# Larger loads, an earlier last K and one end barrier in a load-bound attention decode kernel

## The chip, the cores and the metric

The kernel runs on one core of one Trainium2 chip. Times are device microseconds of that core, medians of several executions. Executions mostly agree within 0.3%, but a few runs are 1 to 2 us longer at an unchanged granted clock. In the views, PE is the matmul engine (PEld its weight load), DVE the vector engine, ACT the scalar engine, POOL the general one, SP the engine that issues the large loads; a q behind a name (SPq) is the engine's instruction sequencer.

## The reference, cut to what matters

```python
# x [4,1,640]; 32 heads of 192; window of the last 2048 keys of 8192; bf16
xn = layernorm(x)
q = xn @ wq                                   # [640, 6144]
o = softmax(q . k_window * 192**-0.5) @ v_window   # for each of 4 x 32 heads
out = x + o @ wo + (silu(xn @ w1) * (xn @ w3)) @ w2
```

K and V of the window are 201 MB, wq and wo 7.9 MB each, w1, w3 and w2 2 MB each: 223 MB are read once for four output rows.

## The kernel before: the parts that the change touches

All large loads go through one queue (`nc.sync`), in program order. Its first load is moved ahead of the start barrier.

```python
def first_load_first(nc):
    for f in nc.python_module().functions:
        head, body = f.blocks[0], f.blocks[1]
        sp = mybir.EngineType.SP
        ...   # the first DMA of this queue goes from body into head, before its drain
```

The loads at the start: `x` on the other queue, wq in three transfers that lie in the three V buffers, then the first two K heads.

```python
    x_sb = const.tile([B, D], BF16, name="x_sb")
    nc.scalar.dma_start(out=x_sb[:], in_=A_x.rearrange("b s d -> (b s) d"))
    wq_v = A_wq.rearrange("(p kc) n -> p kc n", kc=KC)          # KC = 5
    for k0 in range(0, KC, 2):                                  # 2, 2, 1 rows a partition
        n = min(2, KC - k0)
        wt = vpool.tile([P, 2, H * Dh], BF16, tag="vt")
        nc.sync.dma_start(out=wt[:, 0:n, :]..., in_=wq_v[:, k0:k0 + n, :]...)
        ...
    for h in range(KBUFS):                                      # KBUFS = 2
        load_k(h)
```

From x come the layer norm, its transpose, q (60 matmuls with wq), and with q the DVE products with K. Each head has four products (`mult`). The third K load needs the buffer of the first K, so it is issued only after the first head's fourth product:

```python
    for h in range(H):
        u0, ul = h * GQ, h * GQ + GQ - 1                        # GQ = 4
        if h >= KBUFS:
            add((h - KBUFS + 1) * GQ, 0, load_k, h)
        if h < H - 2:
            add(u0 + 2, 0, load_v, h)
```

w1's last 64 rows ("low" rows) are loaded in four small transfers laid out so that only a few of the 16 DMA engines carry them. The end:

```python
    for h in range(H - 2, H):
        add(NU - 6, 0, load_v, h)
    add(NU - 6, 0, w2_load, 0)                                  # W2C: 4, 4, 3, 1 rows
    add(NU - 6, 0, w2_load, 1)
    add(NU - 6, 0, wo_load, NG - 2)                             # wo in groups of 4 heads
    add(NU - 6, 0, wo_load, NG - 1)
    add(NU - 6, 0, w2_load, 2)
    add(NU - 6, 0, w2_load, 3)
```

## Time and profile before

| | before |
|---|---|
| time | 525.7 us |
| span of the profiled run, its time | 523.8, 525.59 us |
| load queue, share of 16 engines | 99.2% |
| DVE, PE busy | 65%, 69% |

From the page of the kernel before: the mean busy share of the DMA engines in 40 slices of 13 us (tenths), what they moved, and the queues with packets, MB and share.

```profile
DMA  9999999999999999999999999999999999999996
GB/s 389 422 443 425 433 431 432 428 433 432 430 435 428 437 418 446 424 437 426 434 434 429 432 434 429 435 427 435 425 437 434 427 437 431 430 434 425 441 418 275
...
q1 hardware_dynamic: 11868, 222.96, 99.2%
q8 instruction: 15, 0.25, 0.2%
```

The engines are full from the second slice to the last but one, so the kernel is bound by its loads. The Trainium skill ("DMA: Bandwidth & Descriptors", Where 436 GB/s comes from) puts the ceiling at 435 GB/s; the middle of this trace, at 428 to 435 in stretches of 20 us, agrees.

From the timeline of the kernel before: start, duration, engine, line, operation; in brackets the idle time before it and what ended it.

```profile
0.00 1.69 SPq L148 DMA_DIRECT2D wt<-in_A_wq_dram  x3
0.79 0.55 ACTq L142 DMA_DIRECT2D x_sb<-in_A_x_dram  x1
...
6.68 0.48 DVE L177 CAST xf<-x_sb 4x640 f32<-4x640 bf16 x1 [3.80 <-DMA x_sb<-in_A_x_dram]
...
41.62 0.54 SPq L125 DMA_DIRECT2D kt<-in_A_k_cache_dram  x1
```

x is 5 KB and is asked for at 0.79 us, but the first operation on it starts at 6.68. The third K load is issued at 41.62.

The end, from the same timeline:

```profile
518.65 0.38 DVE L369 STREAM_TRANSPOSE oT<-og 128x192 bf16<-128x192 bf16 x1
...
519.21 0.98 PE L264 MATMUL acc<-wo_t,oT 128*4 128x320 bf16 x12 [0.47 <-DMA wo_t<-in_A_wo_dram]
520.38 0.71 PE L264 MATMUL acc<-w,hT 128*4 128x320 bf16 x8 [0.19 <-DMA w<-in_B_w_dram]
521.12 0.48 DVE L542 CAST res<-acc 4x320 bf16<-4x320 f32 x1 [2.10 <-PE acc L264]
```

PE waits for loads (wo, then w2) at the very end, and the result copy follows at once. The records of line 569 hold the end barriers: operation, count, shortest/median/longest ns, first and last start.

```profile
L569 SPq DRAIN  x3: 7/7/13, 523.0 to 523.4; - x3
L569 POOLq EVENT_SEMAPHORE  x4: 17/17/17, 523.1 to 523.7; - x4
L569 POOLq EVENT_SEMAPHORE_RANGE_CLEAR  x1: 96/96/96, 523.4 to 523.4; - x1
```

The first barrier stands before the semaphore clear at 523.4, the second after it, up to 523.7.

The trace has a record of every DMA packet, without the engine's number. Weighing each with its steady spacing (about 4.5 ns plus its bytes at 27.2 GB/s, read from packets that follow each other on one engine) gives the work done per engine up to any moment. The **mean lag** is the clock minus that work; it grows only while engines stand still or restart. In the kernel before it is 1.91 us at 40 us, 2.81 at 500. The growth is about that of the instruction fetches: in the packet records those of 16 KB (15 of them) each hold their DMA engine up by about 1.4 us, of which the fetch's own bytes are 0.6 us of work, so that all 15 make 0.75 us spread over 16 engines (an estimate from these figures); five smaller fetches of 8 KB add some more.

### The profile page before, as it was taken

Reading aid. Unit: us, or ns where it says so; the run is one execution under the profiler, and the core shown is the slowest. Engines: PE = TensorE matmul, PEld = TensorE weight load, DVE = VectorE, ACT = ScalarE, POOL = GpSimd, SP = SyncE. Lnnn points to the kernel's source line nnn. Section 1 sums busy time; section 2 is a strip of 40 time slices with the busy share of each in tenths; the row PEclk is TensorE's granted clock in tenths of the full one; section 3 lists DMA queues with packets and bytes.
Section 4 is the critical chain, followed back from the end, with each engine's and each line's share of the span. In section 5 each row is a group of like instructions: output and inputs, shape, how many; then the busy total and the mean of one; then the engine's idle time right before and its main releaser. Section 6 shows DMA issues by size and latency. Waiting matters only on the chain.

```text
span 523.8 us, 4820 instructions
## 1 busy us (share of the span) xinstructions
PE 361.8 (69%) x2336; PEld 75.9 (14%) x1643; DVE 340.9 (65%) x413; ACT 55.8 (11%) x176; POOL 5.6 (1%) x12
## 2 busy tenths in 40 slices
PE   0965866887668776667547768586686876675685
PEld 0100111121111111111111111111111111111122
DVE  3268853687656767577646877466667766667671
ACT  2111111111001110101100111001101110011111
POOL 4000000000000000000000000000000000000000
PEclk9979886898878998789997988889878898889988
DMA  9999999999999999999999999999999999999996
GB/s 389 422 443 425 433 431 432 428 433 432 430 435 428 437 418 446 424 437 426 434 434 429 432 434 429 435 427 435 425 437 434 427 437 431 430 434 425 441 418 275
DMA packets 11904, 223.26 MB, mean 426 GB/s; under 512 B 1332, under 2 KB 1608, under 8 KB 3052
## 3 DMA queue, kind: packets, MB, share of 16 engines
q1 hardware_dynamic: 11868, 222.96, 99.2%
q8 instruction: 15, 0.25, 0.2%
q14 instruction: 5, 0.04, 0.0%
q10 hardware_dynamic: 16, 0.01, 0.0%
HBM read 222.96 MB, written 0.01 MB: 426 GB/s over the span
## 4 chain that ended last, share of the span: by engine, by line
DMA 60%; PE 20%; DVE 15%; ACT 3%; issue 1%; SPq 1%
DMA kt<-in_A_k_cache_dram 44%; PE ps L288 11%; DMA w<-in_B_w_dram 11%; DVE pr L277 10%; DMA vt<-in_A_v_cache_dram 5%; PE po L361 4%; PE qps L243 3%; DVE sc L296 2%; ACT ex L324 1%; DVE z L332 1%; DMA x_sb<-in_A_x_dram 1%; PE mt L318 1%; ACT L324 0%; ACT negm L321 0%; PE mt L305 0%
## 5 line engine op out<-in xcount | busy, mean ns | idle before, releaser
L288 PE MATMUL ps<-pr,idb 128*128 128x512 bf16 x768 | 214.7, 422 | 137.6 <-DVE pr L277 137.5
L277 DVE TENSOR_TENSOR pr<-kt,qbc 128x3072 bf16<-128x3072 bf16 x128 | 223.5, 1746 | 104.0 <-DMA kt<-in_A_k_cache_dram 104.0
L296 DVE TENSOR_REDUCE sc<-ps 128x16 f32<-128x512 f32 x128 | 87.1, 681 | 2.7 <-PE ps L288 2.6
L340 PE MATMUL o_ps<-vt,z 128*8 128x384 bf16 x1024 | 60.5, 380 | 0.2 <-DVE z L332 0.2
L361 PE MATMUL po<-o_sb,sel_w 128*32 128x192 f32 x128 | 49.2, 518 | 0.6 <-ACT o_sb L343 0.6
L340 PEld LDWEIGHTS <-z 128*8 128x8 bf16 x1024 | 26.2, 95 | 98.8 <-issue 89.2
L332 DVE TENSOR_TENSOR z<-ex,mask_b 128x256 bf16<-128x256 bf16 x32 | 13.5, 423 | 38.6 <-ACT ex L324 38.6
L343 ACT COPY o_sb<-o_ps 128x384 f32<-128x384 f32 x32 | 15.3, 478 | 196.9 <-PE o_ps L340 196.9
L313 ACT ACTIVATE gneg<-gmax 1x128 f32<-1x128 f32 x32 | 9.8, 308 | 162.8 <-DVE gmax L310 162.8
L305 PEld LDWEIGHTS mt<-idf,lmax 128*1 128x1 f32 x32 | 3.2, 101 | 127.5 <-issue 125.5
L361 PEld LDWEIGHTS po<-o_sb,sel_w 128*32 128x32 f32 x128 | 13.8, 130 | 29.4 <-issue 27.9
L288 PEld LDWEIGHTS <-idb 128*128 128x128 bf16 x124 | 12.0, 97 | 39.3 <-issue 32.8
L318 PEld LDWEIGHTS mt<-ones_ff,gneg 1*128 1x128 f32 x64 | 9.6, 186 | 47.1 <-issue 43.7
L243 PE MATMUL qps<-wt,xnT 128*128 128x512 bf16 x59 | 14.9, 412 | 0.1
L318 PE MATMUL mt<-ones_ff,gneg 1*128 1x1 f32 x64 | 12.3, 259 | 0.7 <-ACT gneg L313 0.7
L321 ACT COPY negm<-mt 128x1 f32<-128x1 f32 x32 | 5.1, 159 | 70.4 <-PE mt L318 70.4
L310 DVE TENSOR_REDUCE gmax<-mt 1x4 f32<-1x128 f32 x32 | 8.8, 274 | 5.8 <-PE mt L305 5.8
L348 PEld LDWEIGHTS po<-rsum,tot_w 128*32 128x32 f32 x64 | 4.4, 108 | 51.5 <-ACT ex L324 35.4
L249 DVE CAST qbc<-qps 128x512 bf16<-128x512 f32 x6 | 3.8, 684 | 11.7 <-PE qps L243 11.7
L324 ACT ACTIVATE ex<-sc,negm 128x64 bf16<-128x64 f32 x32 | 11.1, 348 | 1.0
L305 PE MATMUL mt<-idf,lmax 128*1 128x128 f32 x32 | 10.9, 340 | 0.0
L199 PE MATMUL xnT_ps<-idb,xn 4*128 4x4 bf16 x5 | 0.4, 178 | 13.4 <-DVE xn L194 13.4
(74 smaller groups left out, 84.4 us busy)
## 6 DMA issues: line engine op xcount, KB each, us to landing
kt<-in_A_k_cache_dram SPq DMA_DIRECT2D x32, 3072.0 KB, 19.1
vt<-in_A_v_cache_dram SPq DMA_DIRECT2D x32, 3072.0 KB, 25.5
wo_t<-in_A_wo_dram SPq DMA_DIRECT2D x8, 960.0 KB, 20.7
wt<-in_A_wq_dram SPq DMA_DIRECT2D x2, 3072.0 KB
w<-in_B_w_dram SPq DMA_DIRECT2D x1, 1920.0 KB
wt<-in_A_wq_dram SPq DMA_DIRECT2D x1, 1536.0 KB, 19.5
w<-in_B_w_dram SPq DMA_DIRECT2D x1, 1536.0 KB
w<-in_B_w_dram SPq DMA_DIRECT2D x2, 640.0 KB
```

What stands on the lines that cost most here:

```text
L243: nc.tensor.matmul(qp[:], lhsT=xnT[:, kc].rearrange("p a b -> p (a b)"), rhs=wq_rows[kc][:, (c0 + i) * QC:(c0 + i + 1) * QC], start=(kc == ...
L277: nc.vector.tensor_tensor(out=pr[:], in0=kts[h][:, g * JQ:(g + 1) * JQ, :], in1=qbc[:, h * Dh:(h + 1) * Dh].unsqueeze(1).to_broadcast([P, ...
L288: nc.tensor.matmul(ps[:], lhsT=idb[:], rhs=pr[:, :, kk * DD:(kk + 1) * DD], start=(kk == 0), stop=(kk == NK - 1))
L296: nc.vector.tensor_reduce(out=scs[h][:, g * JQ:(g + 1) * JQ], in_=pss.pop(u)[:], axis=AX.X, op=ALU.add)
L305: nc.tensor.transpose(out=mt[0:1, 0:P], in_=chs[h][0][:], identity=idf[:])
L313: nc.scalar.activation(out=gneg[:], in_=gmax[:].unsqueeze(1).to_broadcast([1, PB, B]), func=ACTF.Copy, scale=-SCALE)
L318: nc.tensor.matmul(mt[:, P:P + 1], lhsT=gneg[:].rearrange("o p b -> o (p b)"), rhs=ones_ff[:], start=True, stop=True)
L324: nc.scalar.activation(out=ex[:], in_=scs.pop(h)[:], func=ACTF.Exp, bias=negm[:, 0:1], scale=SCALE, accum_out=rsum[:])
L332: nc.vector.tensor_tensor(out=z[:], in0=ex[:].unsqueeze(2).to_broadcast([P, NJ, B]), in1=mask_b[:].unsqueeze(1).to_broadcast([P, NJ, B]), ...
L340: nc.tensor.matmul(o_ps[c * CT:c * CT + 2 * B, :], lhsT=z[:, 2 * jj:2 * jj + 2, :], rhs=vt[:, 2 * jj:2 * jj + 2, :], start=(jj < 4), stop= ...
L343: nc.scalar.copy(out=o_sb[:], in_=o_ps[:])
L361: nc.tensor.matmul(po[sl, 0:Dh], lhsT=sel_w[:, par].rearrange("p a b -> p (a b)"), rhs=o_sb[:, par * Dh:(par + 1) * Dh].rearrange("p (r i) ...
```

## The change

The intent: fewer and larger transfers (wq in two, w2 in one, wo by eight heads instead of four), a last K that does not come behind the third-last V so that the last softmax is done early, a simpler layout of w1's low rows (72 rows in two transfers), and the second end barrier left out.

```diff
+def one_end_barrier(nc):
+    ...  # deletes what follows the semaphore clear in the end block, but for one drain of Pool
-    HG: int = 4,
+    HG: int = 8,
+    FG: int = 4,
@@ wq, in one tile that holds all three V buffers
-    for k0 in range(0, KC, 2):
-        n = min(2, KC - k0)
-        wt = vpool.tile([P, 2, H * Dh], BF16, tag="vt")
+    wq_t = v_all[:, 0:KC * H * Dh].rearrange("p (k n) -> p k n", k=KC)
+    for k0, k1 in ((0, 3), (3, KC)):
@@ the last K into a V buffer, the last V into a K buffer
+        kt = k_buffer() if h < H - 1 else v_buffer()
+        vt = v_buffer() if h < H - 1 else k_buffer()
+    early = {H - 1: (NU - 10, -1)}
@@ low rows of w1
-    for n in range(4):
-        add(4 + 2 * n, 1, w1_low, n)
+    for n in range(2):
+        add(5 + 3 * n, 1, w1_low, n)
@@ the end
-    add(NU - 6, 0, w2_load, 0)  # and 1, 2, 3, with two wo_load between
+    WOC = [0, RPP - 5, RPP - 2, RPP]
+    add(NU - 6, 0, w2_load)
+    for i0, i1 in zip(WOC, WOC[1:]):
+        add(NU - 6, 0, wo_load, NG - 1, i0, i1)
+        add(e, 6, ge_proj, NG - 1, i0, i1, True)
...  # cut: layouts of po, og, oT for eight heads; w1's matmuls
```

## The prediction

> **What bounds the kernel.** The DMA engines. The page's queue part puts the load queue at 99.2% of the 16 engines' time; the stretch table shows 428 to 435 GB/s in every 20 us from 40 to 500 us. The Trainium skill ("DMA: Bandwidth & Descriptors", Where 436 GB/s comes from) gives a ceiling of 435 GB/s; the trace agrees. DVE (65%) and PE (69%) have slack.
>
> From the packet records: 24,576-byte packets start 908 ns apart on an engine, 7,680 ones 287, 1,280 ones 52: about 4.5 ns per packet plus bytes at 27.2 GB/s; a semaphore packet takes 6 ns. With packets weighed so, the engines' mean work lags the clock by 1.9 us from 3 us on (start, fixed), by 0.9 us more from 15 instruction fetches, by nothing else until 517.5. Then engines run out one by one: four with few fetches at 517.2 to 518.6, the others at 519.6 to 520.5. After the last landing (about 520.8) come two projection matmuls (0.30), the copy (0.48), the store and two end barriers, up to 523.8; 1.8 us more lie outside the span.
>
> **What the change does.** It saves no bytes; it adds 24.6 KB (eight w1 rows loaded twice), 0.06 us.
> - Larger packets: wq 128 fewer, wo 256, w2 384: 48 per engine at 4.5 ns, 0.22 us; 7 fewer transfers at 6 ns, 0.04 us. All on the critical path: every engine is full.
> - Low rows of w1: 72, not 64, on the same three engines. Those get about 0.3 us more work; they end at 519.6 to 520.3 now, so they just reach the others' end. At most 0.1 us lost.
> - Last K ahead of three V: same bytes, so the last landing stays. The last K lands about 7 us earlier, its softmax is done before the last V lands (about 511 us), and the transposed output is ready near 517.5 instead of 519.03. Before, that chain already waits for data (0.5 us for wo, 0.2 for w2): safety, not time.
> - Scaling and transposing 384 columns, not 192: 0.4 us longer, inside that slack.
> - After the last landing four matmuls, not two: 0.1 us more (8 took 0.71, 2 took 0.30).
> - Second end barrier: its records run from about 523.45 to 523.75; 0.25 to 0.35 us saved.
>
> Sum: -0.26 +0.06 +0.1 -0.3 = -0.4 us.
>
> **Prediction: 525.3 us, range 524.5 to 525.9.** Faster by over 2%: 0.01; within 2%: 0.98; slower by over 2%: 0.01.
>
> **What would show it.** Load queue still 99%, span about 523.4; 768 fewer large packets; the middle at 428 to 435 GB/s. In the chain of waits the last DMA is a wo piece landing near 520.6, then four matmuls; PE waits for wo, not for the transposed output. After the semaphore clear only one drain.
>
> **What would make it wrong.** Instruction fetches (the skill's "Runtime: NRT & Kernel Launch", Instruction fetch mechanics, says 16 KiB blocks; the trace has 15 of 16,384 bytes) delay single engines by about 1.4 us each; if the shifted program puts them on other engines or near the end, the last landing moves by some tenths. Buffers shared between K, V and wq, or the single wo buffer, could make the in-order load queue wait long enough to starve the engines; I estimate over 8 us of backlog there. If the order near the end exposes the last head's chain, PE would wait for the transposed output.

## The result, and the profile after

The changed kernel takes **526.56 us** (median of six runs, 526.16 to 528.43) against 525.72 (525.61 to 526.16). The ratio is 1.0019 with a 95% interval of 1.0004 to 1.0034: slower by a fifth of a percent, where 525.3 was predicted.

The page and the start and end of the timeline of the changed kernel, in the order of those of before:

```profile
DMA  9999999999999999999999999999999999999996
GB/s 385 426 443 423 432 427 434 427 437 433 432 433 433 431 427 437 424 441 430 429 434 427 439 425 433 431 431 435 431 431 431 431 431 437 429 430 433 428 433 260
...
q1 hardware_dynamic: 10974, 222.98, 99.1%
q8 instruction: 15, 0.25, 0.2%
```

```profile
0.00 1.11 SPq L177 DMA_DIRECT2D v_all<-in_A_wq_dram  x2
0.79 0.54 ACTq L173 DMA_DIRECT2D x_sb<-in_A_x_dram  x1
...
8.10 0.48 DVE L206 CAST xf<-x_sb 4x640 f32<-4x640 bf16 x1 [5.22 <-DMA x_sb<-in_A_x_dram]
...
43.02 0.54 SPq L156 DMA_DIRECT2D kt<-in_A_k_cache_dram  x1
...
517.32 0.58 DVE L401 STREAM_TRANSPOSE oT<-og 128x384 bf16<-128x384 bf16 x1
...
519.17 1.75 PE L295 MATMUL acc<-wo_t,oT 128*4 128x320 bf16 x20 [0.93 <-DMA wo_t<-in_A_wo_dram]
...
521.08 0.44 PE L295 MATMUL acc<-wo_t,oT 128*4 128x320 bf16 x4 [0.17 <-DMA wo_t<-in_A_wo_dram]
...
521.55 0.48 DVE L549 CAST res<-acc 4x320 bf16<-4x320 f32 x1 [3.65 <-PE acc L295]
```

The barriers' records of the changed kernel:

```profile
L576 SPq DRAIN  x2: 7/10/13, 523.5 to 523.5; - x2
L576 POOLq EVENT_SEMAPHORE  x2: 17/17/17, 523.6 to 523.6; - x2
L576 POOLq EVENT_SEMAPHORE_RANGE_CLEAR  x1: 96/96/96, 523.8 to 523.8; - x1
```

What is as predicted: the load queue is as full, 792 data packets fewer (the 768 predicted, of wq, wo and w2, and 24 of w1's low rows), the transposed output is ready 1.1 us sooner (its start plus duration: 517.90 against 519.03), PE waits for wo and not for it, and only a drain follows the clear. What is not: x is first used 1.4 us later, and with it the third K load is issued 1.4 us later; the last load packet ends at 520.77 us instead of 520.49; and 2.16 us instead of 1.79 lie outside the span. For the profiled pair (526.16 and 525.59, a difference of 0.57) the sum closes:

| step | before | changed | difference |
|---|---|---|---|
| last load packet ends | 520.49 | 520.77 | +0.28 |
| from there to the result copy | 0.63 | 0.78 | +0.15 |
| from the copy to the end of the span | 2.68 | 2.45 | -0.23 |
| outside the span | 1.79 | 2.16 | +0.37 |

But this profiled run is the fastest of the six. The median is 0.4 us further up, and something that this trace does not show must make the others slow.

### The profile page after: what moved, and what is told of

It reads as the page before. It is cut to its first block, busy times and chain, and to the rows that moved or that the text cites. A ratio compares the mean times of both kernels' runs of the same rounds, so it can differ in the third digit from the quotient of the medians. Undisturbed runs are those within 1.5% of the kernel's fastest.

```text
span 524.0 us, 4763 instructions
## 1 busy us (share of the span) xinstructions
PE 356.6 (68%) x2327; PEld 74.7 (14%) x1633; DVE 339.6 (65%) x398; ACT 55.9 (11%) x176; POOL 5.5 (1%) x11
## 4 chain that ended last, share of the span: by engine, by line
DMA 61%; DVE 18%; PE 18%; ACT 2%; issue 1%; SPq 0%
DMA kt<-in_A_k_cache_dram 52%; DVE pr L309 12%; PE ps L320 9%; DMA wo_t<-in_A_wo_dram 7%; PE po L393 4%; PE qps L274 3%; DVE sc L328 2%; DMA x_sb<-in_A_x_dram 1%; DVE z L364 1%; ACT ex L356 1%; PE mt L350 1%; ACT L356 0%; PE mt L337 0%; ACT negm L353 0%; DVE xn L223 0%
## 5 line engine op out<-in xcount | busy, mean ns | idle before, releaser
L320 PE MATMUL ps<-pr,idb 128*128 128x512 bf16 x768 | 211.7, 417 | 144.1 <-DVE pr L309 144.1
L309 DVE TENSOR_TENSOR pr<-kt,qbc 128x3072 bf16<-128x3072 bf16 x124 | 216.5, 1747 | 104.6 <-DMA kt<-in_A_k_cache_dram 104.6
L372 PE MATMUL o_ps<-v_all,z 128*8 128x384 bf16 x992 | 54.9, 366 | 0.4 <-DMA v_all<-in_A_v_cache_dram 0.4
L274 PE MATMUL qps<-v_all,xnT 128*128 128x512 bf16 x59 | 15.0, 415 | 0.1
```

Of the source, the lines that this page charges most:

```text
L274: nc.tensor.matmul(qp[:], lhsT=xnT[:, kc].rearrange("p a b -> p (a b)"), rhs=wq_rows[kc][:, (c0 + i) * QC:(c0 + i + 1) * QC], start=(kc == ...
L309: nc.vector.tensor_tensor(out=pr[:], in0=kts[h][:, g * JQ:(g + 1) * JQ, :], in1=qbc[:, h * Dh:(h + 1) * Dh].unsqueeze(1).to_broadcast([P, ...
L320: nc.tensor.matmul(ps[:], lhsT=idb[:], rhs=pr[:, :, kk * DD:(kk + 1) * DD], start=(kk == 0), stop=(kk == NK - 1))
L372: nc.tensor.matmul(o_ps[c * CT:c * CT + 2 * B, :], lhsT=z[:, 2 * jj:2 * jj + 2, :], rhs=vt[:, 2 * jj:2 * jj + 2, :], start=(jj < 4), stop= ...
```

## The experiments

Thirteen runs were made (one of them the changed kernel, unaltered) on four chips, each beside runs of the kernel before on the same chip; all gave right results. The key numbers, the first from the timelines, the lag and the last packet from the packet records of the profiled run, the time as the median of the runs:

| kernel | first op on x | third K issued | mean lag at 40 / 100 us | last packet | time | before |
|---|---|---|---|---|---|---|
| before | 6.68 | 41.62 | 1.91 / 2.05 | 520.49 | 525.72 | |
| changed | 8.10 | 43.02 | 2.01 / 2.15 | 520.77 | 526.56 | 525.72 |
| changed, again | 8.43 | 42.01 | 2.11 / 2.26 | 520.59 | 526.53 | 525.70 |
| before, one end barrier | 6.93 | 41.97 | 1.91 / 2.07 | 520.42 | 525.81 | 525.61 |
| changed, two end barriers | 7.67 | 43.43 | 2.09 / 2.64 | 521.90 | 526.80 | 525.61 |
| changed, wq in three | 6.88 | 41.93 | 1.94 / 2.08 | 520.52 | 525.88 | 525.61 |
| changed, one last wo row | 8.32 | 43.44 | 2.13 / 2.82 | 521.79 | 527.20 | 525.61 |
| changed, x first | 5.53 | 41.31 | 2.01 / 2.15 | 520.56 | 525.98 | 525.64 |
| before, wq in two | 8.29 | 44.49 | 2.02 / 4.03 | 523.36 | 527.99 | 525.64 |
| wq in three, w1 back | 6.87 | 40.80 | 1.89 / 2.03 | 520.11 | 526.12 | 525.64 |
| wq in three, last K back | 6.97 | 42.02 | 1.89 / 2.05 | 520.26 | 525.87 | 525.64 |
| before, x late | 10.04 | 44.03 | 1.98 / 3.07 | 522.41 | 527.69 | 525.71 |
| mended | 4.26 | 40.69 | 1.93 / 2.07 | 520.36 | 525.69 | 525.71 |
| mended, balanced | 4.04 | 40.79 | 1.91 / 7.39 | 531.44 | 536.85 | 525.71 |
| before, x first | 4.44 | 40.28 | 2.01 / 2.15 | 520.50 | 525.60 | 525.70 |

### The first four: the barrier, the size of wq's transfers, the last row

**The kernel before with one end barrier.** Only `one_end_barrier` added.

> The kernel before, with only the second end barrier left out. The prediction's theory (the barrier costs what its records cost): the span falls by 0.25 to 0.35 us and the time with it, to about 525.4 us. The rival (the profiled run after the change has 2.16 us outside its span against 1.79 before): the span falls by about 0.3 us, the time outside it grows by about 0.35 us to 2.15, and the time stays within 0.1 us of before (525.6 to 525.9).

Measured: 525.81 us against 525.61, ratio 0.9999 (0.9987 to 1.0012); span 523.5 against the 523.8 first profiled of before. The time outside the span is 2.15 to 2.21 in all five runs, against 1.75 to 1.84 in the nine of before. The rival is right: the span loses 0.2 to 0.3 us (medians of all runs 523.6 and 523.8) and the time does not; by the median it is 0.2 us longer, within the noise.

**The changed kernel with both end barriers.** `nc.at_finalize(one_end_barrier)` removed.

> The changed kernel with the second end barrier put back. If leaving it out gained 0.3 us of time: about 0.3 us slower than the changed kernel, 526.8. If it only moved the end of the span (rival): the same time as the changed kernel within 0.15 us (about 526.4), a span about 0.3 us longer, and 1.8 us outside the span.

Measured: 526.80 us (525.95 to 527.29), 1.75 to 1.81 outside the span. The time outside the span follows the barrier again. The time itself says nothing about the barrier, for this trace shows what the first profile of the changed kernel did not: the mean lag grows by 0.55 us between 40 and 100 us, in before by 0.14. In the packet records of this run 24,576-byte packets take 950 to 2,366 ns from 46 to 50 us, where the usual is 912; such packets are otherwise seen in the first microseconds and beside instruction fetches, with few exceptions (three other runs have a single one of 1,145 to 1,179 ns near 46 us). I read them as DMA engines that ran dry and start anew; the trace with wq in two, below, shows engines standing still.

**The changed kernel with wq in three transfers.**

```diff
-    for k0, k1 in ((0, 3), (3, KC)):
+    for k0, k1 in ((0, 2), (2, 4), (4, KC)):
```

> The changed kernel with wq in three transfers (two, two and one row per partition), as before. Theory that the longer first packets (36,864 bytes) cost time at the start and leave some DMA engines behind for the whole run: the mean lag at 5 us goes back from 2.0 to 1.9 us, the last landing comes 0.2 to 0.4 us sooner, and the time is 0.2 to 0.4 us below the changed kernel. Rival (the packets' size at the start is of no account): the same within 0.1 us, or 0.05 slower for the packets that it adds.

Measured: 525.88 us (525.75 to 526.06), ratio to before 1.0000 (0.9988 to 1.0013); x used at 6.88, third K at 41.93, no long packets at 46 us, last packet 520.52. One line gives back 0.7 us. The expectation had the amount too small, and its reason was wrong in part: not the lag at the start (1.94 against 2.01 at 40 us) makes most of it.

**One row in the last wo transfer.**

```diff
-    WOC = [0, RPP - 5, RPP - 2, RPP]
+    WOC = [0, RPP - 5, RPP - 1, RPP]
```

> The changed kernel with one row, not two, in the last wo transfer, so that two matmuls and not four follow the last landing. If the four matmuls are 0.14 us of the loss: those after the last landing take 0.30 us instead of 0.44 us, and the time falls by 0.1 to 0.15 us. If the landing is what counts, the time changes by less than 0.05 us.

Measured: 527.20 us, and again a lag that jumps from 2.13 to 2.82 with the third K issued at 43.44. So the time is inconclusive on the row. The trace answers it: from the last packet to the result copy it is 0.79 us as in the changed kernel (0.78), because the matmuls of the four rows before it are still running when the last row lands. The expectation missed.

### What makes the queue run dry

The theory at this point: x lands late because its few packets share their DMA engines with wq's packets, and wq's first packets grew from 24,576 to 36,864 bytes. Everything up to the first products hangs on x, so the third K load comes late. Before it the queue holds wq, two K, one V and most of w1, which by bytes are 19.1 MB; at 431 GB/s (16 packets of 24,576 bytes per 912 ns) and with the lag of 2 us that lasts, by this estimate, until about 46 us. The packet records agree: the packets begun add up to these bytes at 45.94 us in the kernel before and at 45.95 in the changed one. If the third K is not there by then, engines stand still, in a kernel in which they can never catch up.

The packet records show the first step. x's four packets move at 4.80 to 5.35 us in the kernel before, and their semaphore packets 0.96 us later each. In the changed kernel they move at 5.76 to 6.33, the semaphores 1.41 us later: between the two there stands one packet of wq, of 912 or of 1,364 ns. This is what the Trainium skill says ("DMA: Bandwidth & Descriptors", Queues, rings and completion order: an engine takes its queues in turn, a whole packet at a time); this trace agrees, with these two numbers, if one packet record is taken as one packet. It explains the packet between x's data and its semaphore. It does not explain the wait before the data: chained end to start, three or four packets of wq go ahead of x's data on each of the four engines in the kernel before, three in the changed kernel, and only one in the two x-first kernels below. Why as many as three is not shown.

**x first**: in the changed kernel the x load, too, goes ahead of the start barrier.

```diff
-        sp = mybir.EngineType.SP
+        for engine in (mybir.EngineType.SP, mybir.EngineType.Activation):
+            ...  # the first DMA of each queue moves into head
```

> The changed kernel, with the 5 KB load of x issued before the start barrier, beside the first wq load, instead of after it; wq stays in two transfers. Theory (late x): in the changed kernel x lands late because its packets wait behind the first 36,864-byte packets of wq; everything up to the first use of K hangs on x, so the third K load is issued at 43.0 to 43.4 us, and the load queue runs dry near 46 us in most runs. With x early: the first op on x starts before 5 us instead of 7.7 to 8.3, the third K load is issued before 41.5 us, no long packets at 46 to 50 us, mean lag at 100 us 2.05 to 2.2 us, and the time is 525.6 to 525.9, 0.6 to 0.9 below the changed kernel. Rival (the long first packets cost time by themselves, or leave engines behind from the start): the time stays at 526.3 to 526.8, with the third K load early all the same.

Measured: 525.98 us (525.76 to 526.11), against 526.56 for the changed kernel, and just above the 525.6 to 525.9 expected; ratio to before 1.0002 (0.9990 to 1.0014), so not told apart from it. The rival would have kept it at 526.3 or more with the same long packets. x is used from 5.53 us, a little later than the 5 us expected; the third K is out at 41.31. From its timeline:

```profile
0.00 1.42 SPq L177 DMA_DIRECT2D v_all<-in_A_wq_dram  x2
0.12 0.54 ACTq L173 DMA_DIRECT2D x_sb<-in_A_x_dram  x1
...
5.53 0.48 DVE L206 CAST xf<-x_sb 4x640 f32<-4x640 bf16 x1 [2.35 <-DMA x_sb<-in_A_x_dram]
...
41.31 0.54 SPq L156 DMA_DIRECT2D kt<-in_A_k_cache_dram  x1
```

**wq in two transfers, alone**, in the kernel before (one V tile for all three buffers, as the change has it; nothing else).

> The kernel before, with only the wq load in two transfers (three rows and two rows per partition, in one V tile). Theory (this part alone makes the loss, through x): x lands 1 us later, the third K load is issued at 43.0 to 43.5 us instead of 41.6, packets of 1 to 2.4 us at 46 to 50 us in the trace, and the time is 0.5 to 1.2 us above before (526.2 to 526.9). Rival (the loss comes from the end: w1, last K, wo by eight heads): the time stays within 0.2 us of before.

Measured: 527.99 us (526.16 to 528.54), ratio 1.0034 (1.0019 to 1.0049). This one part of the change loses more than the whole change does, and twice to four times what was expected (0.5 to 1.2 us), because the third K goes out at 44.49 us and not at 43.0 to 43.5. The lateness of x alone does not explain that, for x is used only 0.2 us later than in the changed kernel: PE was slower as well. The first matmuls of q start 0.43 us apart in every trace and the later ones 0.22, and here the slow pace holds for 13 of them, in the changed kernel for 8. Its timeline, and the table of stretches (length; busy time of PE, PEld, DVE, ACT and POOL with counts; clock, DMA share, GB/s) from 44 to 50 us:

```profile
8.29 0.48 DVE L180 CAST xf<-x_sb 4x640 f32<-4x640 bf16 x1 [5.41 <-DMA x_sb<-in_A_x_dram]
...
44.49 0.54 SPq L125 DMA_DIRECT2D kt<-in_A_k_cache_dram  x1
```

```profile
44.00:46.00 2.00, 1.46 (x6) 0.00 (x0) 2.00 (x3) 0.00 (x0) 0.00 (x0) 1.00 1.12 429
46.00:48.00 2.00, 1.22 (x6) 0.08 (x1) 1.97 (x4) 0.00 (x0) 0.00 (x0) 1.00 0.69 241
48.00:50.00 2.00, 1.04 (x7) 0.10 (x1) 2.00 (x4) 0.31 (x1) 0.00 (x0) 1.00 1.15 369
```

The same stretches of the kernel before:

```profile
44.00:46.00 2.00, 1.47 (x7) 0.18 (x2) 1.97 (x3) 0.00 (x0) 0.00 (x0) 1.00 1.11 461
46.00:48.00 2.00, 1.57 (x8) 0.19 (x2) 2.00 (x4) 0.31 (x1) 0.00 (x0) 1.00 1.13 477
48.00:50.00 2.00, 1.31 (x8) 0.20 (x2) 0.83 (x1) 1.74 (x4) 0.00 (x0) 1.00 0.97 418
```

A packet counts here by its start, so single stretches swing by 10%; 241 against 477 GB/s is no swing. It is the dry queue, 2 us long, that the 13-us slices of a page hide. In its packet records 16 engines have a packet under way until 45.5 us, 10 at 47 us, and 16 again at 48.75; in the kernel before all 16 throughout.

**x late, with wq in three transfers.** In the kernel before the x load goes into the load queue, behind the first wq transfer.

```diff
-    nc.scalar.dma_start(out=x_sb[:], ...)
+        if k0 == 0:   # in the loop of wq's transfers
+            nc.sync.dma_start(out=x_sb[:], ...)
```

> The kernel before with nothing changed but the place of the 5 KB load of x: it is put into the load queue behind the first wq transfer, so it lands about 4 us later; wq keeps its three transfers and packets of at most 24,576 bytes. Theory (only the lateness of x counts, not the size of wq's packets): the first op on x starts near 11 us instead of 6.7, the third K load is issued near 45.9 us, later than in any run so far, and the queue runs dry for longer than in the kernel before with wq in two (44.5 us, where the mean lag grew by 2.0 us): mean lag at 100 us 5 to 6.5 us, time 528 to 530 us. Rival (long packets are what hurts): within 0.5 us of before.

Measured: 527.69 us (526.75 to 528.41), ratio 1.0029 (1.0015 to 1.0043), third K at 44.03 us, lag at 100 us 3.07. No packet of wq is longer than before, and still the queue runs dry. So the lateness of x is enough by itself. The size was over-estimated (528 to 530): I had moved the third K load by as much as x, but the first operation on x moved by 3.4 us and the third K by 2.4.

The four traces with the third K at 43.43 us or later (43.43, 43.44, 44.03, 44.49) have the jump in the lag near 47 us; of the others, at 43.02 or earlier, only the failed layout below shows a jump, later and of another cause. The kernel before stands 1.8 us from that edge, the changed kernel 0.4 us. What moves a run towards it is x and the pace of PE together: the slow pace at the start of q lasts for 7 matmuls in the profile of the kernel before, 8 and 6 in the two of the changed kernel, 12 with both barriers, 9 with one last row. So the kernel with both barriers is over the edge although its x is used earlier (7.67) than in the changed kernel (8.10). By these traces the late x takes most of the slack away, and PE's pace, which differs between executions, can take the rest. What sets that pace these runs do not show.

### The rest of the change

**wq in three, w1 as before.** The w1 part of the kernel before in the changed kernel.

> The changed kernel with wq in three transfers and, besides, the w1 loads as before (64 low rows in four transfers instead of 72 in two). If the 0.3 us of extra load on three DMA engines sets the last landing: the last packet ends at 520.2 to 520.3 us instead of 520.5 and the time falls by 0.2 us against wq in three alone (525.7). If it does not reach the end of the others, as predicted: no change within 0.1 us (525.8 to 525.9).

Measured: 526.12 us, but with two of five runs at 527.2; the other three are 525.79, 525.87 and 526.12. In the trace the last packet ends at 520.11, 0.4 us before that of the kernel with wq in three alone (520.52), so the new w1 layout may cost some tenths at the end. But the next kernel, with the new w1, ends at 520.26. It stays open.

**wq in three, last K where it was.**

```diff
-    early = {H - 1: (NU - 10, -1)}
+    early = {}
-        kt = k_buffer() if h < H - 1 else v_buffer()
+        kt = k_buffer()
...   # the same for V, and the end slots of before
```

> The changed kernel with wq in three transfers and the last K load where it was, after V of head 29. The transposed output of the last heads is then ready near 519.4 us instead of 517.7, and 24 projection matmuls (1.4 us) must follow it, so the PE ends them near 520.9 to 521.2 at best. If the earlier last K only buys slack: the same time within 0.1 us (525.8 to 525.9). If eight heads at once need it: 0.2 to 0.5 us slower (526.1 to 526.4), and before the last matmuls the PE waits for the transposed output.

Measured: 525.87 us (525.74 to 526.04) against 525.88 with the last K ahead. The transposed output is ready at 516.96 us, over 2 us before what this text expected, and sooner than in the changed kernel (517.90), and PE waits for wo. The earlier last K buys nothing in time here, as the prediction said.

**Mended**: x first, wq in three, both barriers, w1 as before, wo's last transfers of 8, 3 and 1 rows. Kept are w2 in one transfer, wo by eight heads, and the last K ahead.

> The changed kernel with what the runs so far blame taken back: x loaded early, wq in three transfers, both end barriers, w1 as before, and the last wo transfers of 8, 3 and 1 rows. Kept: w2 in one transfer, wo by eight heads, last K ahead. Theory (nothing else costs): no dry queue, mean lag at 100 us 2.0 to 2.1, last packet at 520.1 to 520.3 us, result copy 0.65 us after it, time 525.4 to 525.6, 0.05 to 0.25 below before. Rival (another part of the change costs too): 525.8 or more.

Measured: 525.69 us (525.62 to 526.19), ratio to before 0.9994 (0.9980 to 1.0008). Not told apart from before, and between the theory's 525.4 to 525.6 and the rival's 525.8. The last packet (520.36) comes 0.13 us sooner than in before (520.49), but the copy follows after 0.79 us, not 0.65: with wo as the last load the end stays as long as in the changed kernel. In this profile what the larger packets save, the end takes.

**Mended and balanced.** In the kernel before five engines have ended by 518.6 us (the texts say four) and eleven end at 519.6 to 520.5. Chaining the packets end to start, with the order of their sizes as a check, gives the reason: seven engines carry two of the 16-KB instruction fetches each and end at 519.7 to 520.5, and three with neither a fetch nor low rows of w1 end at 517.2 to 517.5; the engines with w1's low rows are among the late ones. This kernel moves loads from those to the rest:

```diff
-    KM, LE, LI, LS = KC - 1, 3, 4, 3
+    KM, LE, LI, LS = KC - 1, 8, 2, 2
...
+        for p0, p1 in ((0, P - 16), (P - 16, P - 8), (P - 8, P)):
+            nc.sync.dma_start(out=wt[p0:p1]...)     # w3: 112, 8 and 8 partitions
```

> As the mended kernel, but the loads of w1's low rows and of 16 of w3's 128 partitions are laid out for eight DMA engines instead of three and sixteen, to take work from the eight that also fetch instructions (in before these end at 520.0 to 520.5 us, four of the others at 517.2 to 518.6). If those eight set the last landing: the last packet ends at 519.9 to 520.1 us and the time is 525.0 to 525.3, 0.3 to 0.5 below the mended kernel. If the ends are not set by this balance: no change within 0.1 us.

Measured: 536.85 us. It failed, and what the balance is worth cannot be read from it: w3's 15,360-byte packets took 591 to 1,909 ns instead of 573. The mean lag grows by 7.8 us from 88 to 108 us, the stretch of w3, and in the whole run by some 9 us more than in the kernel before. Packets of 24,576 bytes in that stretch are slow too (up to 2,848 ns), with all 16 engines busy. The page's row shows it as one slice at 227 GB/s:

```profile
GB/s 384 435 434 426 416 412 388 227 434 426 434 435 426 435 431 434 430 430 435 427 432 434 431 434 427 435 429 435 428 429 438 427 435 428 433 432 433 432 427 190
```

Whether a better balance would help, and why this stretch is so slow (w3's cut into 112, 8 and 8 partitions, or something that goes with it), was not tested further.

### Are the slow runs dry queues?

**The changed kernel once more**, unaltered.

> The changed kernel once more, unaltered, for a second profile and five more times. Theory (the dry queue near 46 us is what makes most of its runs slow, and the first profiled run, the fastest of six, just escaped it with its third K load at 43.0 us): times of 526.2 to 527.3 again; if this profiled run takes over 526.4 us, its third K load is issued at 43.2 us or later and its trace has packets of 1 to 2.4 us at 46 to 50 us; if it takes under 526.3, it has none. Rival (a slow run has another cause): a profiled run over 526.4 us without such packets, or under 526.3 us with them.

Measured: 526.53 us (525.99 to 528.15), ratio 1.0018 (1.0002 to 1.0034): the loss is there again. The profiled run was again the fastest, 525.99, with the third K at 42.01 us and no long packets, as the theory has it for a run under 526.3. Why its third K came 1 us sooner than in the first profile, at a later x: PE was granted its full clock in this run from 32 to 36 us, in the first profile 0.70, and the products of the first head wait for PE; the slow pace at the start of q was also shorter, 6 matmuls instead of 8. The slow runs of the unaltered changed kernel were never caught in a profile; that they are dry queues rests on the two kernels with the same start that were (both barriers; one last row). Whether it is the only cause of slow runs stays open: the kernel before has some, and so has the kernel with wq in three and w1 back (two of five at 527.2, its third K at 40.80 us in the profiled run, well before the edge), and no profile caught one of these either.

**The kernel before with x first.**

> The kernel before, with only the load of x issued before the start barrier. In before the third K load, at 41.6 us, is early enough, so slack is all that an earlier x buys: first op on x near 4.3 us, third K load at 39 to 41 us, median within 0.15 us of before (525.5 to 525.8), and no run over 526.5 us, if those of before (5 of some 37) are dry queues too. Rival (before loses to a late x in each run as well): 525.4 or less.

Measured: 525.60 us (525.51 to 526.25), ratio 0.9997 (0.9985 to 1.0010). x is used at 4.44, the third K is out at 40.28, and the time is the same: slack that the kernel before does not need in most runs. No run is over 526.5 us; of the 42 runs of before in the experiments, 7 are. Five runs are too few to say that this is more than luck.

## Why the prediction was wrong

- **The bound and the packets: right.** The load queue is as full, and the engines' work by the packet records is 516.31 us instead of 516.52 (predicted 0.20 less).
- **The step that failed: the start was taken as fixed, and the load queue as never short.** The prediction put the start's lag down as "(start, fixed)", counted for wq only the packets that it saves, and put the reserve of the load queue where buffers are shared at "over 8 us of backlog". It did name the in-order load queue as a danger, but not its thin place, which is at 46 us, before the third K load, and which hangs on x. When the third K is issued there are 4.3 us of backlog in the kernel before (45.94 less 41.62) and 2.9 in the changed one, not over 8. Two transfers for wq make x 1.4 us late through the larger packets ahead of it; with that the third K comes within 0.4 us of the edge at 43.4 us, and a little more lateness of x or of PE puts it over, as in the two traces with the same start that show the dry queue (43.43 and 43.44). That the slow runs of the unaltered changed kernel are of this kind is not shown by a profile of one. Wq in two alone costs 2.4 us (527.99 against 525.64), and in the changed kernel taking the lateness away (x first, or wq in three) gives back 0.6 to 0.7 us.
- **The second end barrier: wrong.** Predicted -0.25 to -0.35. The span loses 0.2 to 0.3 us and the time outside it grows by at least as much: 2.11 to 2.21 us in every run of the kernels with one barrier, 1.74 to 1.87 in those with two (1.91 to 1.95 where x goes into the load queue, for a reason not looked into). The kernel before without it took 525.81 against 525.61.
- **The matmuls after the last landing: right in direction, too small in size.** Predicted +0.1; 0.63 us from the last packet to the copy became 0.78.
- **Last K ahead, and 384 columns at once: no time, as predicted,** by the run that puts the K back. In the profiled run the output was ready 1.1 us sooner, less than the 1.5 predicted, and even that is not shown to come from the earlier K: with the K put back the output is ready at 516.96, in the kernel before with x first at 516.85, and the two profiles of the changed kernel differ by 1.4 us (517.90 and 516.47). That this number came near was luck.
- **Low rows of w1: open.** The last packet of the changed kernel ends 0.28 us later instead of 0.2 sooner although its work is 0.2 us less; 0.1 is lag from the start, and the rest is the spread of the engines' ends. The runs do not settle whether w1's rows make it.

What is left of the loss with x first is 0.34 us by the medians (525.98 against 525.64; by the ratio it is not clear of noise), which the end (0.15) and the longer first packets (0.1 of lag) are large enough to make, together with the second barrier if it costs the 0.2 us that its median says; that sum is not shown term by term.

## What to carry to other kernels

In a load-bound kernel look for the moment at which the queue has least left, not at its mean: here it was the first reuse of a buffer, and it hung on the chain from the first small input. Here a tiny load behind large packets waited for them, so try to issue it first, and read the start in stretches of 2 us, for the page's slices hide a dry queue of that length. And count a saving at the end of the span only when the time shows it, not the span.

## What the Trainium skill lacked or had wrong

- "Runtime: NRT & Kernel Launch", Instruction fetch mechanics, calls the cost of crossing a 16 KiB boundary "mostly hidden" and says nothing of the DMA engine that carries the fetch. In this kernel, bound by its loads, 14 of the 15 fetches hold up the engine that carries them by 1.41 to 1.44 us each in the chains of packets (the last one, among small packets, was not read), and the seven engines that carry two end at 519.7 to 520.5 us, where engines without any end as early as 517.2.
- "DMA: Bandwidth & Descriptors", Where 436 GB/s comes from, says that for loads from HBM the HBM side (about 358 GB/s) binds, while the single-core table of the same page reaches 425 GB/s. One core alone read 426 GB/s over the whole span here, and 428 to 435 in stretches of the middle, near the table's figure and not that of the HBM side.
- The same page, Specifications, gives about 27 GiB/s per engine. The packets here run at 27.2 GB/s, which is 25.3 GiB/s, plus about 4.5 ns each.
- The same page states the turn-taking by packets but not what it does to a small load: three or four packets of wq went ahead of x's, and between x's packet and its semaphore packet stood one more, 0.96 us at 24,576 bytes and 1.41 us at 36,864.
- No page gives the cost of cutting a load unevenly over the partitions: in the run with w3 in 112, 8 and 8 partitions packets of 15,360 bytes took 591 to 1,909 ns instead of 573. The cause was not isolated.
- No page says what the second end barrier is worth: 1.74 to 1.87 us lie outside the span with it, 2.11 to 2.21 without, and the span is 0.2 to 0.3 us shorter.
